# The order of the units in the product stage of a long-convolution block: early copies in the first group, whole pairs at the end of later groups

## The chip, the cores and the metric

The kernel runs on one core of a Trainium2 chip. The time is the device time of one execution in microseconds (us). Before the change it is 208.33 us, the median of three runs (207.98 to 208.43).

A core has TensorE (PE, matmuls, with its weight loads shown apart as PEld), VectorE (DVE), ScalarE (ACT), GpSimd (POOL) and SyncE (SP). Each takes its instructions in order, and semaphores tie the engines together. Matmuls write PSUM, eight banks per partition; ScalarE and VectorE read it.

## The reference

The block has two halves. The first is a gated long convolution over S = 2048 tokens and D = 512 channels, the second a dense ReLU layer pair with 1376 hidden units:

```python
k_shift = sum over 4 taps of shifted k * shift_k
kv = k_shift * v
y = irfft(rfft(kv padded to 2S) * rfft(ssm_k padded to 2S))[:S] + kv * ssm_D
h = x + layernorm(x) * y
out = h + relu(layernorm(h) @ w1) @ w2
```

The convolution is causal and runs along the tokens, for each channel by itself. What matters here is the product of the two spectra in the middle of it.

## The kernel before

The transforms are written as matmuls with tables of sines. The work goes in stages:

1. Tables, the four taps (`taps`) and a first transform step (`stage1`) of the filter into the tile `BK` and of `kv` into the tile `BX`. `stage1` runs 64 matmuls per call and casts the two PSUM buffers of a call out on ScalarE and VectorE (lines 273 and 275).
2. The product stage (lines 410 to 491). It carries out the second transform step of both and multiplies the two, and is the part that is changed.
3. The inverse transform (`inv1`, line 577, PSUM tile `psi`; then `inv2`, line 668, PSUM tile `pz`), with the weights `w1` centred beside it.
4. The dense layers, `mlp1` and `mlp2` (lines 680 and 696).

The product stage works in eight groups, c = 0 to 7, each with six units: four pairs u0 to u3 (`pairs`, line 437) and two sums s0 and s1 (`sums`, line 459). "Pair" is the kernel's own word for such a unit. A unit owns one PSUM buffer of two banks. In each of the two banks the left half takes the unit's transform K of the filter, from `BK`, and the right half its transform X of the data, from `BX`. A pair has a step K and a step X, of four matmuls each. A sum has four steps, K1, K2, X1 and X2, where 1 and 2 are two ways of assigning the array's row halves; a no-op on TensorE waits for the matmuls of one way before the other way begins.

`times(unit)` then multiplies the two: `forms` copies the K half out of PSUM to SBUF on ScalarE (line 423, tiles `ktu` and `kts`, two buffers each), and VectorE multiplies the X half, still in PSUM, with that copy (line 471). The product of a pair goes back into `BK`, into rows that neighbouring units' K steps read; the product of a sum goes into `BX`. So a product waits for all K steps that read its rows. Writing K and X below always means these halves; "copy u3" and "product u3" are the two instructions of `times` for u3.

There are four PSUM buffers of this kind. A new unit takes the one that was given back first, in the order of the products in the text, and its first matmul waits for that product.

The order of all this is written out by hand in two strings. A word such as `u3K` or `s0X1` is a step on TensorE, and a word such as `=u3` is the copy and the product of that unit. Each engine gets its instructions in the order of the string, and `FIRST` is for group 0, `OTHER` for groups 1 to 7:

```python
FIRST = "s0K2 u1K s1K2 s0K1 u0K s1K1 s0X1 u1X =u1 s0X2 =s0 s1X1 u0X =u0 s1X2 =s1 u2K u2X u3K =u2 u3X =u3"
OTHER = "s0K1 s0X1 u0K u0X s0K2 u1K =u0 s0X2 =s0 s1K1 s1X1 u1X =u1 s1K2 s1X2 =s1 u3K u2K u3X =u3 u2X =u2"
```

Beside the groups GpSimd makes the sum tables (`sum_tables`, line 383) for a group three later, and in three groups adds up rows of `w1` (line 416). At the end of the stage `column_means` runs four matmuls (line 500), and then the inverse transform begins.

Of the kernel before, what the change touches and what calls it, by code (L numbers as in the profile page):

```python
# [56 lines left out]
def kernel(  # L57
# [33 lines left out]
    early = pl.push("early", side="right")  # L91
# [287 lines left out]
    def sum_tables(c):  # L379
        ks = slice(4 * c, 4 * c + 4)  # L380
        for dp, pq in enumerate(halves):
            for i, op in ((0, ALU.subtract), (1, ALU.add)):
                nc.gpsimd.tensor_tensor(out=smc[pq, c % 3, i, :, 64 * dp:64 * dp + 64], in0=st[pq, ks, 64:128].bitcast(F32),  # L383
                                        in1=st[pq, ks, 0:64].bitcast(F32), op=op)
# [29 lines left out]
    def add_chunks(step):  # L414
        o, a, b = ((wsum, w1[:, 0, :], w1[:, 1, :]), (wpair, w1[:, 2, :], w1[:, 3, :]), (wsum, wsum.bitcast(F32), wpair.bitcast(F32)))[step]
        nc.gpsimd.tensor_tensor(out=o, in0=a, in1=b, op=ALU.add)
# [4 lines left out]
    def forms(ps, tag):  # L421
        kt = prod.tile([P, 2, 256], F32, tag=tag, name=tag, bufs=2)
        nc.scalar.copy(out=kt[:], in_=ps)  # L423
        return kt
# [40 lines left out]
                ways[way, dp] = last[dp]  # L465
        return do, ps, "kts", BXs[:, :, k1:k1 + 2, :].rearrange("p g k x -> p k g x")

    def times(unit):
        do, ps, tag, o = unit
        kt = forms(ps[:, :, 0:256], tag)  # L470
        nc.vector.tensor_tensor(out=o, in0=ps[:, :, 256:512].rearrange("p b (g x) -> p b g x", x=8),  # L471
                                in1=kt[:].rearrange("p b (g x) -> p b g x", x=8), op=ALU.mult)

    FIRST = "s0K2 u1K s1K2 s0K1 u0K s1K1 s0X1 u1X =u1 s0X2 =s0 s1X1 u0X =u0 s1X2 =s1 u2K u2X u3K =u2 u3X =u3"
    OTHER = "s0K1 s0X1 u0K u0X s0K2 u1K =u0 s0X2 =s0 s1K1 s1X1 u1X =u1 s1K2 s1X2 =s1 u3K u2K u3X =u3 u2X =u2"
    for c in range(8):
        units = {}
        for step in (OTHER if c else FIRST).split():  # L480
            if step[0] == "=":
                times(units[step[1:]])
                continue
            u = step[:2]
            if u not in units:
                units[u] = (pairs if u[0] == "u" else sums)(4 * c + (1 if u[0] == "u" else 2) * int(u[1]))
            units[u][0](step[2:])
        if c + 3 < 8:
            sum_tables(c + 3)
        if c in (2, 4, 5):  # L490
            add_chunks(max(c - 3, 0))
# [289 lines left out]
```

## Time and profile before

| what | value |
|---|---|
| median of three runs | 208.33 us |
| the profiled execution | 208.08 us |
| its span, first to last instruction | 206.3 us |
| mean granted TensorE clock | 0.994 |
| TensorE busy | 198.5 us, 96% of the span |
| VectorE, ScalarE, GpSimd busy | 69%, 57%, 34% |
| copies of line 423 | 48, 589 ns each |
| products of line 471 | 48, 685 to 688 ns each |

In a row of the timeline stand the start (us from the span's start), the time it took, engine, line, operation, what it writes and reads, the shapes and how many instructions were merged; in brackets the idle time of the engine before it and what ended it. The step of a row is found by its place in the string: in `OTHER`, a row `us<-BK` is s0K1, s0K2, s1K1 or s1K2, and `u<-BX` the X of a pair. Matmuls are pipelined: a row's time is longer than the distance to the next row, and it is the distance that counts.

### The profile page before, as it was taken

The page shows a single profiled execution, that of the slowest core. Times are in us where ns is not written, and L with a number is a line of the kernel's source. Part 1 is how long each engine was busy: PE and PEld are TensorE (multiplying, and loading weights), DVE is VectorE, ACT ScalarE, POOL GpSimd, SP SyncE. Part 2 cuts the span into 40 slices and gives each one's busy share as a digit, 9 for nine tenths or more (in the row PEclk, how much of TensorE's full clock was granted, in tenths as well). Part 3 has the DMA queues.
Part 4 walks back from the last instruction along what each step waited for, and adds up shares of the span by engine and source line. Part 5 has one row for each costly group of instructions (what it writes and reads, how often), then busy time and mean ns, then how long its engine had stood idle before and what let it go on. Part 6 is the DMA issues. An engine that isn't in the chain of part 4 may idle for free.

```text
span 206.3 us, 4591 instructions
## 1 busy us (share of the span) xinstructions
PE 198.5 (96%) x1861; PEld 139.0 (67%) x1869; DVE 142.5 (69%) x246; ACT 117.2 (57%) x190; POOL 69.4 (34%) x118
## 2 busy tenths in 40 slices
PE   8999999999999999999999999999999999999991
PEld 2575556877899999899998944466444844444460
DVE  5989898698689999997743775899098641361130
ACT  5776789787677877777691078404950065026300
POOL 7963801991557996032003032042102200002000
PEclk9999999999999999999999999999999999999997
DMA  5999970001700000035515999997906805110011
GB/s 161 344 209 191 214 122 3 0 5 22 257 0 3 0 3 3 0 108 98 101 39 176 277 195 105 204 148 135 124 12 130 142 25 105 29 57 16 0 51 51
DMA packets 47819, 19.93 MB, mean 97 GB/s; under 512 B 42710, under 2 KB 46264, under 8 KB 47800
## 3 DMA queue, kind: packets, MB, share of 16 engines
q1 hardware_dynamic: 44144, 16.15, 40.2%
q10 hardware_dynamic: 3656, 3.51, 5.6%
q8 instruction: 14, 0.23, 0.5%
q14 instruction: 5, 0.04, 0.1%
HBM read 7.02 MB, written 2.10 MB: 44 GB/s over the span
## 4 chain that ended last, share of the span: by engine, by line
PE 87%; DVE 7%; ACT 2%; DMA 1%; issue 1%; DVEq 0%; ACTq 0%
PE ps1m L680 19%; PE ps2m L696 18%; PE psi L577 11%; PE us L459 8%; PE ps L300 8%; PE u L437 7%; PE pz L668 7%; PE pkv L335 7%; PE pst L284 2%; DVE E L44 1%; DVE BK L471 1%; DMA wsh<-in_A_shift_k_dram 1%; DVE G L222 1%; DVE G L220 1%; ACT ktu L423 1%
## 5 line engine op out<-in xcount | busy, mean ns | idle before, releaser
L682 ACT ACTIVATE M<-ps1m 128x512 bf16<-128x512 f32 (+1 forms) x44 | 25.1, 595 | 49.4 <-PE ps1m L680 39.0
L696 PE MATMUL ps2m<-M 128*128 128x512 bf16 (+3 forms) x183 | 38.5, 366 | 0.2
L696 PEld LDWEIGHTS <-M 128*128 128x128 bf16 (+1 forms) x187 | 18.3, 98 | 19.9
L680 PEld LDWEIGHTS <-w 128*128 128x128 bf16 (+1 forms) x176 | 17.4, 100 | 19.9
L383 POOL TENSOR_TENSOR smc<-st 64x256 fp32r<-64x256 f32 x32 | 22.7, 730 | 10.8 <-PE us L459 10.0
L539 POOL TENSOR_SCALAR rstd<-mv 128x4 f32<-128x4 f32 x8 | 2.2, 276 | 70.1 <-DVE mv L537 70.1
L698 DVE SCALAR_TENSOR_TENSOR M<-ps2m,rstd,M 128x512 bf16<-128x512 f32 (+1 forms) x13 | 9.2, 707 | 23.2 <-PE ps2m L696 14.7
L471 DVE TENSOR_TENSOR BK<-u,ktu 128x512 fp32r<-128x512 f32 x32 | 21.3, 688 | 4.6 <-ACT ktu L423 3.3
L423 ACT COPY ktu<-u 128x512 f32<-128x512 f32 x32 | 18.1, 589 | 7.5 <-PE u L437 6.1
L577 PE MATMUL psi<-inv,BK 128*128 128x128 f32 x128 | 21.1, 255 | 0.0
L577 PE MATMUL psi<-inv,BX 128*128 128x256 f32 x64 | 20.5, 338 | 0.1
L577 PEld LDWEIGHTS psi<-inv,BK 128*128 128x128 f32 x128 | 19.7, 197 | 0.0
L680 PE MATMUL ps1m<-M,w 128*128 128x512 bf16 (+1 forms) x88 | 19.3, 379 | 0.0
L680 PE MATMUL ps1m<-xT,w 128*128 128x512 bf16 (+1 forms) x88 | 19.3, 379 | 0.0
L459 PE MATMUL us<-BK,smc 64*128 64x256 f32 x128 | 15.0, 313 | 0.4 <-ACT BX L273 0.4
L459 PE MATMUL us<-BX,smc 64*128 64x256 f32 x128 | 13.2, 284 | 0.0
L437 PE MATMUL u<-BK,st 64*128 64x256 f32 x128 | 12.9, 294 | 0.3 <-DVE BK L471 0.3
L577 PEld LDWEIGHTS psi<-inv,BX 128*128 128x128 f32 x64 | 12.1, 196 | 0.5 <-DVE BK L471 0.4
L535 DVE BATCH_NORM_STATS2 st<-M 128x6 f32<-128x512 bf16 x20 | 12.3, 678 | 0.0
L315 ACT CAST BK<-ps 128x512 fp32r<-128x512 f32 x16 | 9.3, 584 | 5.1 <-PE ps L300 3.4
L437 PE MATMUL u<-BX,st 64*128 64x256 f32 x128 | 11.9, 281 | 0.0
L654 DVE TENSOR_TENSOR qT<-pz,qT 128x2048 bf16<-128x2048 f32 x2 | 4.6, 2292 | 9.9 <-DMA qT<-M 5.8
(126 smaller groups left out, 408.4 us busy)
## 6 DMA issues: line engine op xcount, KB each, us to landing
E<-in_A_ssm_k_dram SPq DMA_DIRECT2D x1, 2048.0 KB
out_dram<-M ACTq DMA_DIRECT2D x15, 128.0 KB
w<-in_B_w_dram SPq DMA_DIRECT2D x1, 1376.0 KB
M<-in_B_w_dram ACTq DMA_DIRECT2D x1, 1280.0 KB
M<-in_A_q_dram SPq DMA_DIRECT2D x8, 128.0 KB
xh<-in_A_q_dram SPq DMA_DIRECT2D x4, 128.0 KB
xr<-in_A_q_dram SPq DMA_DIRECT2D x4, 128.0 KB
out_dram<-M ACTq DMA_DIRECT2D x2, 64.0 KB
```

The costliest lines, as they stand in the source:

```text
L300: nc.tensor.matmul(out=pss[rp][:, gi // 2, :, gi % 2, :], lhsT=fl[rows, 2 * g:2 * g + 2, :].rearrange("p d n -> p (d n)"), rhs=f[rows].rea ...
L335: nc.tensor.matmul(out=ps[:, i, :], lhsT=wdiag[:, r0 + i, j, :], rhs=kT[c][:, r0 + i, 16 - j:CH + 16 - j], start=(j == 0), stop=(j == KS - 1))
L383: nc.gpsimd.tensor_tensor(out=smc[pq, c % 3, i, :, 64 * dp:64 * dp + 64], in0=st[pq, ks, 64:128].bitcast(F32), in1=st[pq, ks, 0:64].bitcas ...
L423: nc.scalar.copy(out=kt[:], in_=ps)
L437: nc.tensor.matmul(out=ps[:, dp, 256 * x:256 * x + 256], lhsT=t[pq], rhs=cols((BK, BX)[x], pq, k1, i), start=not begun, stop=(i == 1), til ...
L459: mm = nc.tensor.matmul(out=ps[:, k % 2, 256 * x:256 * x + 256], lhsT=smc[pq, k // 4 % 3, i, k % 4, :], rhs=cols((BK, BX)[x], pq, k, i), s ...
L471: nc.vector.tensor_tensor(out=o, in0=ps[:, :, 256:512].rearrange("p b (g x) -> p b g x", x=8), in1=kt[:].rearrange("p b (g x) -> p b g x", ...
L577: nc.tensor.matmul(out=o if part == 0 else o[:, P * part - P:P * part], lhsT=src[:, g // 2, :, g % 2::2].rearrange("p c r -> p (c r)"), rh ...
L668: nc.tensor.matmul(out=pz[:, i, :, a:a + w, :].rearrange("p (s r) a n -> p s r (a n)", s=2), lhsT=ax[rho][:, n2 // 2, n2 % 2, :], rhs=ecor ...
L680: nc.tensor.matmul(out=ps1[:fsz, :].rearrange("p (i t) -> p i t", i=4), lhsT=w1[:, c, fc * P:fc * P + fsz], rhs=hT[sc][:, :, c, :], start= ...
L682: nc.scalar.activation(out=h1T[:fsz, fc, :], in_=ps1[:fsz, :], func=ACT.Relu)
L696: nc.tensor.matmul(out=ps2, lhsT=h1T[:ksz, fc, i * P:(i + 1) * P], rhs=w2[:ksz, fc, d0:d0 + w], start=(fc == 0), stop=(fc == NFC - 1))
```

## The change

`times` is split: `copy_k(unit)` is the copy alone, and `times` takes a copy that was made before. A new word `+u0` in the order makes that copy at its place, and the later `=u0` is then only the product.

In the first group the pairs u0 and u1 now go first with their K steps, and each is followed by its copy. The sums follow way by way as in later groups, and u3 goes ahead of u2. In later groups one thing is changed: u3X moves in front of u2K, so that the order at the end is u3K u3X u2K u2X, and copy and product u3 stand behind u2K. The numbers of matmuls, copies and products are the same.

```diff
-    def times(unit):
+    def copy_k(unit):
         do, ps, tag, o = unit
-        kt = forms(ps[:, :, 0:256], tag)
+        return forms(ps[:, :, 0:256], tag)
+
+    def times(unit, kt=None):
+        do, ps, tag, o = unit
+        kt = copy_k(unit) if kt is None else kt
         nc.vector.tensor_tensor(out=o, in0=ps[:, :, 256:512].rearrange("p b (g x) -> p b g x", x=8),
                                 in1=kt[:].rearrange("p b (g x) -> p b g x", x=8), op=ALU.mult)
...
-    FIRST = "s0K2 u1K s1K2 s0K1 u0K s1K1 s0X1 u1X =u1 s0X2 =s0 s1X1 u0X =u0 s1X2 =s1 u2K u2X u3K =u2 u3X =u3"
-    OTHER = "s0K1 s0X1 u0K u0X s0K2 u1K =u0 s0X2 =s0 s1K1 s1X1 u1X =u1 s1K2 s1X2 =s1 u3K u2K u3X =u3 u2X =u2"
+    FIRST = "u0K +u0 u1K +u1 s0K1 s0X1 u0X s0K2 =u0 u1X =u1 s0X2 =s0 s1K1 s1X1 u3K s1K2 s1X2 =s1 u2K u3X =u3 u2X =u2"
+    OTHER = "s0K1 s0X1 u0K u0X s0K2 u1K =u0 s0X2 =s0 s1K1 s1X1 u1X =u1 s1K2 s1X2 =s1 u3K u3X u2K =u3 u2X =u2"
     for c in range(8):
-        units = {}
+        units, early = {}, {}
         for step in (OTHER if c else FIRST).split():
+            if step[0] == "+":
+                early[step[1:]] = copy_k(units[step[1:]])
+                continue
             if step[0] == "=":
-                times(units[step[1:]])
+                times(units[step[1:]], early.pop(step[1:], None))
                 continue
```

## The prediction

> **What bounds the kernel now.** I read the page first (busy shares, then the chain that ended last), then the chain in order of time, then the product stage instruction by instruction, engine by engine. The page's rows of busy time and of the chain by engine:
>
> ```profile
> span 206.3 us, 4591 instructions
> PE 198.5 (96%) x1861; PEld 139.0 (67%) x1869; DVE 142.5 (69%) x246; ACT 117.2 (57%) x190; POOL 69.4 (34%) x118
> PE 87%; DVE 7%; ACT 2%; DMA 1%; issue 1%; DVEq 0%; ACTq 0%
> ```
>
> TensorE is on the chain for 87% of the span, so time that it loses inside the product stage counts. The stage runs from 49.6 us to 86.7 us; its end in the chain (start, us, what):
>
> ```profile
> 84.04 0.59 ACT ktu L423
> ...
> 84.65 0.69 DVE BK L471
> 85.34 0.60 DVE BX L471
> ...
> 85.96 0.70 DVE BK L471
> ...
> 86.71 23.23 PE psi L577 x192
> ...
> 109.96 0.29 DVE BX L275
> ...
> 110.60 7.64 PE pz L668 x64
> ```
>
> The stage ends not with a matmul but with copy u1, product u1, product s1, product u3 of the last group; the first inverse matmul at 86.71 waits for product u3, whose PSUM buffer it takes. From there TensorE runs without a break for 23.23 us and nearly so to the end. So what brings that point forward shortens the span one for one. One steady group, c=3, with the end of c=2 (timeline by engine; a step is 4 matmuls, that is two pairs; an x8 row is two steps):
>
> ```profile
> 61.96 0.41 PE L437 MATMUL u<-BX,st 64*128 64x256 f32 x4
> 62.20 0.50 PE L459 MATMUL us<-BK,smc 64*128 64x256 f32 x4
> 62.54 0.40 PE L459 MATMUL us<-BX,smc 64*128 64x256 f32 x4
> ...
> 63.27 0.65 PE L437 MATMUL u<-BX,st 64*128 64x256 f32 x8
> 63.87 0.51 PE L459 MATMUL us<-BK,smc 64*128 64x256 f32 x4
> ...
> 64.43 0.46 PE L437 MATMUL u<-BK,st 64*128 64x256 f32 x4
> 64.73 0.40 PE L437 MATMUL u<-BX,st 64*128 64x256 f32 x4
> 64.97 0.41 PE L459 MATMUL us<-BK,smc 64*128 64x256 f32 x4
> ...
> 65.69 0.50 PE L459 MATMUL us<-BK,smc 64*128 64x256 f32 x4
> 66.03 0.41 PE L459 MATMUL us<-BX,smc 64*128 64x256 f32 x4
> ...
> 68.17 0.48 PE L459 MATMUL us<-BK,smc 64*128 64x256 f32 x3
> ...
> 62.41 0.58 ACT L423 COPY ktu<-u 128x512 f32<-128x512 f32 x1 [0.26 <-PE u L437]
> 63.01 0.58 ACT L423 COPY kts<-us 128x512 f32<-128x512 f32 x1
> 63.72 1.08 ACT L423 COPY ktu<-u 128x512 f32<-128x512 f32 x2
> ...
> 63.03 0.69 DVE L471 TENSOR_TENSOR BK<-u,ktu 128x512 fp32r<-128x512 f32 x1 [0.15 <-ACT ktu L423]
> 63.64 0.68 DVE L471 TENSOR_TENSOR BX<-us,kts 128x512 fp32r<-128x512 f32 x1
> 64.34 1.29 DVE L471 TENSOR_TENSOR BK<-u,ktu 128x512 fp32r<-128x512 f32 x2
> ```
>
> A free-running step takes 0.24 us (64.73 to 64.97). Steps that take more follow a wait: s1K1 takes 0.34 (65.69 to 66.03), as does the change of way at 62.20. So a wait that ends late costs about 0.10 even when TensorE is not seen idle; the row's own length tells it, 0.50 for 0.41. There are four PSUM buffers, handed on in the order of the products: s0 of the next group takes u1's, u0 takes s1's, u1 takes u3's, s1 takes u2's. Read with that, the rows give a loop: u1X starts at 61.96; its copy at 62.41; product u1 at 63.03 to 63.72; s0K1 of the next group at 63.87, 1.91 after u1X began. Only from s0K1 to the next u1X does TensorE set its own pace, and there s1K1 loses 0.10 on product u2 (second of the two at 64.34, end 65.63). The group takes 68.17-63.87 = 4.30; 32 pairs at 0.12 would be 3.9.
>
> **Later groups (c=1 to 7): u3X goes ahead of u2K.** Nothing is added: same 64 matmuls, 6 copies, 6 products, no DMA, no GpSimd instruction; nothing moves past the queues of SyncE or GpSimd. u3X ends 0.24 earlier, u2K 0.24 later, u2X as before. Copy u3 waits for u3X (63.72 is 0.45 after the row at 63.27, as 62.41 is 0.45 after 61.96), so it is ready at 63.48. ScalarE's copies follow each other at about 0.48 (two in 1.08), so after copy s1 at 63.01 it starts at 63.49 and ends about 64.08. VectorE is then the one that is late: back to back its products follow at 0.61 (63.03, 63.64), so product u3 starts at 64.25 instead of 64.34: 0.09 earlier, not 0.24. Product u2 follows 0.61 later and ends at 65.54 instead of 65.63. u2K reads the rows of BK that product u3 writes, and so must be done first: it now ends about 63.7, well ahead of 64.25.
>
> s1K1 of the next group at 65.69 then has its buffer 0.15 ahead instead of 0.06. Is that enough to lose the 0.10? In c=3, u1K found its buffer free about 0.18 ahead (product u3 at 64.34 plus 0.69 is 65.03) and ran in 0.24:
>
> ```profile
> 65.21 0.41 PE L437 MATMUL u<-BK,st 64*128 64x256 f32 x4
> 65.45 0.41 PE L459 MATMUL us<-BX,smc 64*128 64x256 f32 x4
> ```
>
> u0K at 64.43 had 0.11 (product s1 ends 64.32) and took 0.30, a loss of 0.06. 0.15 lies nearer the first: I take 0.00 to 0.02 left of the 0.10. Bounds: all of it goes, or (as u0K) 0.06 stays. Once s1K1 is 0.10 earlier, u1X, its copy, its product and the next s0K1 are too: the loop hands it on. The steps that lost it, u1K of c=2 and s1K1 of c=2 and of c=7:
>
> ```profile
> 60.78 0.50 PE L437 MATMUL u<-BK,st 64*128 64x256 f32 x4
> 61.38 0.51 PE L459 MATMUL us<-BK,smc 64*128 64x256 f32 x4
> ...
> 82.99 0.51 PE L459 MATMUL us<-BK,smc 64*128 64x256 f32 x4
> ```
>
> s1K1 does so in all six groups from c=2 to c=7 (in c=1 it doesn't): 6 x 0.10 = 0.60. u1K of c=2, by the same 0.09 of product u3, adds 0.10. At the end, product u3 starts right behind product s1 with the same 0.09, so the psi stage starts 0.10 earlier still. Sum 0.80, between 0.40 and 0.90.
>
> **First group.** What was and is available (TensorE, ScalarE, VectorE; the first ACT row is the last cast of the stage before, the DVE row is product s1):
>
> ```profile
> 49.60 0.51 PE L459 MATMUL us<-BK,smc 64*128 64x256 f32 x4
> ...
> 50.74 0.76 PE L459 MATMUL us<-BK,smc 64*128 64x256 f32 x8 [0.39 <-ACT BX L273]
> ...
> 53.94 0.50 PE L437 MATMUL u<-BK,st 64*128 64x256 f32 x4 [0.31 <-DVE BK L471]
> ...
> 55.23 0.51 PE L459 MATMUL us<-BK,smc 64*128 64x256 f32 x4
> ...
> 55.79 0.46 PE L437 MATMUL u<-BK,st 64*128 64x256 f32 x4
> ...
> 49.68 1.01 ACT L273 CAST BX<-ps 128x1024 fp32r<-128x1024 f32 x1 [0.22 <-PE ps L300]
> 52.58 0.59 ACT L423 COPY ktu<-u 128x512 f32<-128x512 f32 x1 [1.88 <-PE u L437]
> ...
> 55.00 0.68 DVE L471 TENSOR_TENSOR BX<-us,kts 128x512 fp32r<-128x512 f32 x1
> ```
>
> Now u0K and u1K fill 49.60 to 50.2 (two steps, as before). The third unit still waits for the cast to 50.69, so the gap before 50.74 stays. ScalarE copies u0 at 50.71 to 51.30 and u1 to 51.78, in time in which it was idle (1.88 us). From here each pair is put 0.12 behind the last, and 0.10 is added where a wait has just ended. s0K1 50.74 and s0X1 51.09 run; u0X must wait for the copy of its own bank: 51.35 and 0.10 more. s0K2 51.69, u1X 51.94, s0X2 52.18, s1K1 52.42, s1X1 52.66, u3K 52.91 (buffer of u0, product from about 52.13 to 52.82; loses 0.07), s1K2 53.22, s1X2 53.47, u2K 53.71, u3X 53.95, u2X 54.19: TensorE ends at 54.43 where s0K1 stood at 55.23, 0.8 less. But VectorE gives only part of it on: product s1 needs s1X2 (53.59 for its last pair, 0.32 to the copy, 0.59 copy) and ends at 55.21 instead of 55.68, so u0K of c=1 waits until 55.27, where it stood at 55.79. It then loses 0.10 rather than the 0.06 of c=3, which leaves 0.48. s1K1 of c=1 had its buffer just in time; product u2, behind product s1 in VectorE's queue, comes nearly as much earlier, but the lead stays narrow, and up to another 0.10 goes there. I take 0.40.
>
> Bounds: the copy-before-X wait isn't shown in this trace in that direction. Below: u0X waits for both copies (51.78), 0.48 more, and the first group gains nothing. Above: no wait at all; what u0X gains is mostly lost again in u0K's wait for product s1, so 0.45. I take the value between, 0.40, where each X waits for its own unit's copy, because the copies of before wait for no more than their own unit's X.
>
> The Trainium skill bears on this (PSUM — Partial Sum Buffer, "PSUM bank collisions raise a hardware error"): guard PSUM by bank, not by address, since a matmul write and a read in one bank collide even in other columns. It speaks against an early copy: K and X of a unit share their banks, so X stands still while K is copied. The trace agrees in the direction that it shows: copies read K alone, yet each starts after X. By that rule the first group gains 0.40, by guarding addresses about 0.45.
>
> **Sum.** 0.80 + 0.40 = 1.20 us. The profiled execution took 208.08 us (span 206.3 and 1.8 around it): 206.9. The median of the runs is 0.25 above that execution, which would make it 207.1; I say 207.0.
>
> **Rivals.**
> (1) One part only. The wait at s1K1 stays because VectorE frees the buffer too late (0.06 left in six groups: 0.4 less), or the early units' X wait for both copies (0.4 less): 207.4. For it: the lead of 0.15 lies between two rows that decide differently.
> (2) No change. The stage ends earlier but the gain is lost before the end: the psi stage is followed at 109.96 by casts and at 110.60 by pz, which a DMA or a cast could hold. Against it: those casts wait for psi itself. Time 208.1.
> (3) Slower: X straight behind its own K, into the same two banks, restarts as a change of way does (62.20 to 62.54, 0.10 lost). Place: u3X and u2X in seven groups. From u1X to the next s0K1 TensorE has seven steps, 7 x 0.24 + 0.10 = 1.78 of the loop's 1.91, so 0.05 a step would cost nothing. At 0.10 a step they take 1.98, and each group loses most of what s1K1 gave: about 207.5. At 0.15 the gain of the first group goes too, about 208.2; from there it is slower, and at 0.20, 0.27 over the loop less the 0.10 of s1K1 in seven groups, less the first group's 0.40: 208.9. Against it: u0X stands behind u0K already and takes 0.24 (64.73 to 64.97).
>
> **How the numbers follow.** A measurement of this kernel can't tell less than about 0.2% (0.42 us) from no change. Forecast (both parts, 206.6 to 207.4): 0.62. Rival 1: 0.22, faster too. Rival 2: 0.08. Rival 3: 0.08. Faster 0.84, within 0.2% 0.08, slower 0.08. The range 206.4 to 207.8 holds the forecast with its upper bound (0.90+0.45) and a little spread below, and rival 1 with both losses (0.8 less) above; rivals 2 and 3 are left out.
>
> **What would show it.** s0K1 of c=1 near 54.5 and u0K of c=1 near 55.3; copy u3 of later groups starting about 0.49 behind copy s1, not 0.71; steps s1K1 at 0.24 in c=2 to 7; group length 4.20 instead of 4.31; psi from about 85.5 instead of 86.71, and still 23.2 long. Wrong if the s1K1 step stays at 0.34 (rival 1), if psi starts early and pz not (2), or if u3X or u2X take 0.34 (3).

## The result and the profile after

The changed kernel takes 207.38 us, the median of 20 runs (207.13 to 208.31), against 208.31 us for the kernel before (207.98 to 209.15). The ratio is 0.9963, with a 95% interval of 0.9953 to 0.9973: 0.4% faster, clear of no change. The profiled execution took 207.31 us, with a span of 205.2 us, 1.1 us less than before.

From the page of the changed kernel, its span and the chain that ended last by engine:

```profile
span 205.2 us, 4606 instructions
...
PE 90%; DMA 4%; ACT 2%; DVE 1%; issue 1%; SPq 0%
```

VectorE has gone from 7% of the chain to 1%, but most of that is not the change. Of VectorE's 14.1 us on the chain before, 10.4 lie ahead of the product stage, nearly all of them in the first 13 us; there the chain of the new profile runs over a DMA of 8.16 us instead, and the first `ps` matmuls start at the same moment (15.35 and 15.36). Within the product stage VectorE's part falls from 2.7 us to 0.7. The end of the stage and what follows it, in the chain in order of time (start, us, what):

```profile
83.57 0.97 PE u L437 x16
84.54 1.04 PE pm L507 x4
...
85.60 23.19 PE psi L584 x192
...
109.45 7.64 PE pz L675 x64
```

The inverse transform starts at 85.60 instead of 86.71, lasts as long as before, and `pz` starts 1.15 earlier. What was won before 85.60 is still there at the end. The stage now ends with TensorE's own matmuls (line 507) as the last link, where before it was copy u1 and three products. Product u3 ends at about 85.54 and those matmuls at 85.57, so this is a tie rather than a new bound.

A steady group of the changed kernel, c=3, with the end of c=2 (timeline of TensorE; the distance from row to row counts):

```profile
61.45 0.43 PE L437 MATMUL u<-BX,st 64*128 64x256 f32 x4
...
62.29 0.41 PE L437 MATMUL u<-BK,st 64*128 64x256 f32 x4
62.53 0.41 PE L437 MATMUL u<-BX,st 64*128 64x256 f32 x4
62.77 0.42 PE L437 MATMUL u<-BK,st 64*128 64x256 f32 x4
63.01 0.41 PE L437 MATMUL u<-BX,st 64*128 64x256 f32 x4
63.38 0.51 PE L459 MATMUL us<-BK,smc 64*128 64x256 f32 x4
...
65.20 0.41 PE L459 MATMUL us<-BK,smc 64*128 64x256 f32 x4
65.45 0.40 PE L459 MATMUL us<-BX,smc 64*128 64x256 f32 x4
...
67.60 0.51 PE L459 MATMUL us<-BK,smc 64*128 64x256 f32 x4
```

s1K1 (65.20) takes 0.25 where it took 0.34. u3K, u3X, u2K and u2X follow each other at 0.24. The group takes 67.60-63.38 = 4.22 instead of 4.30. Copies s1 and u3 of c=2 (timeline of ScalarE) show where the change acts: copy u3, the first of the second row, starts 0.48 behind copy s1, where it was 0.71.

```profile
62.52 0.59 ACT L423 COPY kts<-us 128x512 f32<-128x512 f32 x1
63.00 1.08 ACT L423 COPY ktu<-u 128x512 f32<-128x512 f32 x2
```

The loop itself is unchanged: from u1X at 61.45 to the next s0K1 at 63.38 are 1.93 us, and TensorE waits there, as s0K1 starts 0.37 behind u2X, where a step without a wait follows at 0.24.

### The profile page after: what moved, and what is told of

It reads as the page before. It is cut to its first block, busy times and chain, and to the rows that moved or that the text cites. A ratio compares the mean times of both kernels' runs of the same rounds, so it can differ in the third digit from the quotient of the medians.

```text
span 205.2 us, 4606 instructions
## 1 busy us (share of the span) xinstructions
PE 197.6 (96%) x1869; PEld 138.1 (67%) x1869; DVE 141.9 (69%) x246; ACT 116.4 (57%) x190; POOL 69.4 (34%) x118
## 4 chain that ended last, share of the span: by engine, by line
PE 90%; DMA 4%; ACT 2%; DVE 1%; issue 1%; SPq 0%
PE ps1m L687 19%; PE ps2m L703 19%; PE psi L584 11%; PE us L459 8%; PE ps L300 8%; PE pz L675 7%; PE u L437 7%; PE pkv L335 7%; DMA E<-in_A_ssm_k_dram 4%; PE pst L284 3%; PE pm L507 1%; ACT xfl L287 0%; ACT BX L273 0%; DVE BX L475 0%; DVE BK L312 0%
## 5 line engine op out<-in xcount | busy, mean ns | idle before, releaser
L459 PE MATMUL us<-BK,smc 64*128 64x256 f32 x128 | 14.5, 302 | 0.6 <-ACT BX L273 0.6
L437 PE MATMUL u<-BK,st 64*128 64x256 f32 x128 | 13.5, 290 | 0.2 <-DVE BX L475 0.2
L437 PE MATMUL u<-BX,st 64*128 64x256 f32 x128 | 13.0, 281 | 0.0
```

The costliest lines, as they stand in the source:

```text
L437: nc.tensor.matmul(out=ps[:, dp, 256 * x:256 * x + 256], lhsT=t[pq], rhs=cols((BK, BX)[x], pq, k1, i), start=not begun, stop=(i == 1), til ...
L459: mm = nc.tensor.matmul(out=ps[:, k % 2, 256 * x:256 * x + 256], lhsT=smc[pq, k // 4 % 3, i, k % 4, :], rhs=cols((BK, BX)[x], pq, k, i), s ...
```

## The experiments

The question was which of the two parts brings how much, whether the mechanism in each is the one that was named, and where the rest of the first group's time went. Each run was compared with the kernel before on the same chip.

**The two parts alone.** First the new `FIRST` with the old `OTHER`:

```diff
-    OTHER = "... =s1 u3K u3X u2K =u3 u2X =u2"
+    OTHER = "... =s1 u3K u2K u3X =u3 u2X =u2"
```

> The new order of the first group with the old order of the later groups. Theory of the prediction (two parts that add): TensorE ends the first group about 0.7 us earlier, VectorE's queue of products hands on about 0.3 of it (u0K of c=1 near 55.45 instead of 55.79), s1K1 of c=2 to 7 keeps its 0.34 us, the span is about 206.0 and the inverse transform starts near 86.4. Rival (the early copies bring nearly all of the 1.1 us of span): span 205.2 to 205.4. Rival (the first group's gain is lost again in later groups): span 206.3, as before.

Measured: 207.90 us, ratio 0.9978 (0.9968 to 0.9988), span 205.9. The opposite, the old `FIRST` with the new `OTHER`:

> The old order of the first group with u3X ahead of u2K in the later groups. Theory: s1K1 of c=2 to 7 takes 0.24 us, a group 4.24 instead of 4.31, the inverse transform starts near 85.9, the span is about 205.5 (0.8 less than before). Rival (all of it is the first group's): span 206.3 and groups of 4.31 us.

Measured: 207.53 us, ratio 0.9965 (0.9951 to 0.9979), span 205.4. The step s1K1 and the one behind it in c=3, and the start of the inverse transform, with the first group's order alone, from TensorE's timeline and from the chain:

```profile
65.40 0.51 PE L459 MATMUL us<-BK,smc 64*128 64x256 f32 x4
65.75 0.41 PE L459 MATMUL us<-BX,smc 64*128 64x256 f32 x4
```

```profile
86.40 23.18 PE psi L584 x192
```

and with the later groups' order alone, from the same two views:

```profile
65.45 0.41 PE L459 MATMUL us<-BK,smc 64*128 64x256 f32 x4
65.69 0.42 PE L459 MATMUL us<-BX,smc 64*128 64x256 f32 x4
```

```profile
85.83 23.22 PE psi L584 x192
```

The wait at s1K1 is there with the old order (0.35) and gone with the new (0.24). At the start of the inverse transform the first part is worth 86.71-86.40 = 0.31 us, the second 0.88; together 1.19, against 1.11 with both. They add up to within 0.1, as was held, and most comes from the later groups. That the early copies bring nearly all of it is refuted.

**Is it the earlier end of copy u3?** In the kernel before, with both old orders, copy u3 was made shorter instead of earlier in groups 1 to 7. The kernel then leaves out one bank's K, and product u3 takes the other bank's for both:

```diff
+        if half:
+            kt = prod.tile([P, 2, 256], F32, tag=tag, name=tag, bufs=2)
+            nc.scalar.copy(out=kt[:, 0, :], in_=ps[:, 0, 0:256])
+            k = kt[:, 0, :].rearrange("p (g x) -> p g x", x=8).unsqueeze(1).to_broadcast([P, 2, 32, 8])
+        else:
...
-                times(units[step[1:]])
+                times(units[step[1:]], c > 0 and step == "=u3")
```

> The kernel before, both orders old; in groups 1 to 7 copy u3 takes only one of its two banks (256 columns fewer, left out of the computation: product u3 uses one bank's K for both). Theory: what the new order of the later groups brings is nothing but an earlier end of copy u3, so that product u3 starts behind product s1 in VectorE's queue (0.09 us earlier) and s1K1 no longer waits. A copy that is 0.2 us shorter does the same with u3X where it was: s1K1 in 0.24, a group 4.24, the inverse transform near 85.85, span 205.4 as with the later groups' order alone. Rival (the gain is that X follows its own K, or that u2K comes later and no longer meets product s0): span 206.3, groups of 4.31.

Measured: 207.42 us, ratio 0.9960 (0.9943 to 0.9978), span 205.4. Its copies s1 and u3 (timeline of ScalarE, with line 423 for a whole copy and 472 for the half one):

```profile
62.78 0.58 ACT L423 COPY kts<-us 128x512 f32<-128x512 f32 x1
63.60 0.37 ACT L472 COPY ktu<-u 128x256 f32<-128x256 f32 x1 [0.24 <-PE u L437]
```

Its products s1 and u3 (timeline of VectorE):

```profile
63.41 0.68 DVE L477 TENSOR_TENSOR BX<-us,kts 128x512 fp32r<-128x512 f32 x1
64.01 1.29 DVE L477 TENSOR_TENSOR BK<-u,ktu 128x512 fp32r<-128x512 f32 x2
```

The step s1K1 and the one behind it (timeline of TensorE), and the start of the inverse transform (chain):

```profile
65.46 0.40 PE L459 MATMUL us<-BK,smc 64*128 64x256 f32 x4
65.70 0.41 PE L459 MATMUL us<-BX,smc 64*128 64x256 f32 x4
```

```profile
85.83 23.22 PE psi L582 x192
```

The copy starts no earlier than in the kernel before (0.82 behind the start of copy s1, there 0.71) but takes 0.37, and product u3 follows product s1 at 0.60. The inverse transform starts at 85.83, the same as with the later groups' new order. So the new place of u3X or u2K isn't itself what helps: it is that copy u3 ends before VectorE is free for its product.

**Is the loop what sets a group's length?** In the changed kernel copy u1 was made twice in groups 1 to 7:

```diff
+        if twice:
+            nc.scalar.copy(out=kt[:], in_=ps[:, :, 0:256])
...
+    TWICE = "=u1"
...
-                times(units[step[1:]], early.pop(step[1:], None))
+                times(units[step[1:]], early.pop(step[1:], None), c > 0 and step == TWICE)
```

> The changed kernel; in groups 1 to 7 ScalarE makes copy u1 twice, one behind the other (0.48 us more). Theory (a group's length is the loop u1X, copy u1, product u1, s0K1 of the next group): each group becomes 0.4 to 0.48 longer, 4.24 to about 4.67, span 208.2 to 208.6. Rival (TensorE's own steps or VectorE's queue set the length, and a copy on ScalarE, which is busy for under 3.6 of 4.3 us, is hidden): span 205.2 to 205.6.

Measured in one run: 211.2 us, span 209.4, 4.2 us more than the changed kernel, or 0.60 in each of seven groups. ScalarE's timeline, with copy u0, copy s0, the two copies u1 (lines 423 and 476) and copy s1:

```profile
65.87 0.59 ACT L423 COPY ktu<-u 128x512 f32<-128x512 f32 x1 [0.71 <-PE u L437]
66.60 0.59 ACT L423 COPY kts<-us 128x512 f32<-128x512 f32 x1
67.33 0.59 ACT L423 COPY ktu<-u 128x512 f32<-128x512 f32 x1
67.94 0.59 ACT L476 COPY ktu<-u 128x512 f32<-128x512 f32 x1
68.43 0.59 ACT L423 COPY kts<-us 128x512 f32<-128x512 f32 x1
```

TensorE's timeline, with u1X of the same group and s0K1 of the next:

```profile
66.87 0.41 PE L437 MATMUL u<-BX,st 64*128 64x256 f32 x4
69.40 0.51 PE L459 MATMUL us<-BK,smc 64*128 64x256 f32 x4 [0.58 <-DVE BK L477]
```

A copy that was held to be hidden by the rival, on an engine that still stands idle in every group (0.71 here), lengthens the kernel by all that it takes. All of it lies in the stretch from u1X to the next s0K1, 2.53 for 1.93 in the changed kernel; from s0K1 (64.57) to u1X (66.87) it is 2.30, for 2.31 there. The loop sets the length. The size was expected at up to 0.48 a group and is 0.60, so the span lies above the expected 208.2 to 208.6: the second copy starts 0.61 behind the first, which writes the same tile, while the copy behind it, into another tile, follows at 0.49.

**What the early copies bring.** The words `+u0` and `+u1` were taken out of the new `FIRST`:

```diff
-    FIRST = "u0K +u0 u1K +u1 s0K1 s0X1 u0X s0K2 =u0 ...
+    FIRST = "u0K u1K s0K1 s0X1 u0X s0K2 =u0 ...
```

> The changed kernel without the two early copies: in the first group the words +u0 and +u1 are taken out, so copies u0 and u1 are made where their products stand. Theory (the early copies matter, since ScalarE has nothing else to do from 50.7 us and copy u0 would else wait for u0X): product u0 starts about 0.2 us later than in the changed kernel, the whole row of products with it, span 205.4 to 205.5. Rival (the order alone brings the first group's gain, the early copies nothing): span 205.2, as the changed kernel. Rival (the bank wait makes an early copy a loss): span under 205.1.

Measured: 207.64 us, ratio 0.9974 (0.9958 to 0.9989), span 205.3; the inverse transform starts at 85.79, 0.19 later than in the changed kernel. The first product starts at 52.52 instead of 52.27 (rows of VectorE's timelines, first without and then with early copies):

```profile
52.52 1.29 DVE L475 TENSOR_TENSOR BK<-u,ktu 128x512 fp32r<-128x512 f32 x2 [1.59 <-ACT ktu L423]
```

```profile
52.27 1.29 DVE L475 TENSOR_TENSOR BK<-u,ktu 128x512 fp32r<-128x512 f32 x2 [1.32 <-PE us L459]
```

The direction and the size in the trace are those expected. The span of the profiled execution (205.3, expected 205.4 to 205.5) is a little below; over all 12 runs the median span is 205.45, against 205.15 over the 20 of the changed kernel, which were not taken beside them. In the times alone, 0.19 us can't be told from nothing. With the early copies the first product waits no longer for a copy but for the matmuls of s0K2, whose rows it overwrites.

**Does X wait for the copy of its bank?** In the changed kernel this can't be seen, since u0X comes late enough. So u0X was put right behind u1K:

```diff
-    FIRST = "u0K +u0 u1K +u1 s0K1 s0X1 u0X s0K2 =u0 ...
+    FIRST = "u0K +u0 u1K +u1 u0X s0K1 s0X1 s0K2 =u0 ...
```

> The changed kernel, with u0X in the first group put right behind u1K, ahead of s0K1 and s0X1, so that it meets copy u0 while that runs. Theory (X waits for the copy of its own banks): u0X starts 0.05 to 0.1 us after copy u0 ends (near 51.25, where BX is ready at 51.0), and s0K1, s0X1 follow it; span 205.6 to 205.9. Rival (the wait goes by address): u0X near 51.0, as soon as BX is ready. Rival (X waits for both copies): u0X near 51.75.

Measured in one run: 207.81 us, span 205.7. u0X in the timeline of TensorE, and copies u0 and u1 in that of ScalarE:

```profile
51.24 0.51 PE L437 MATMUL u<-BX,st 64*128 64x256 f32 x4 [0.96 <-ACT ktu L423]
```

```profile
50.59 1.08 ACT L423 COPY ktu<-u 128x512 f32<-128x512 f32 x2
```

Copy u0 runs from 50.59 to about 51.18, and u0X starts at 51.24; the profile names the copy as what ended the wait. Copy u1 ends at 51.67, so X waits for its own unit's copy alone. The data in `BX`, which u0X needs too, were complete at 50.95, when VectorE's last cast ended (48.50+2.45), so they don't account for the start at 51.24. The Trainium skill (PSUM — Partial Sum Buffer, "PSUM bank collisions raise a hardware error") asks for a guard by bank, since a write and a read collide there even in other columns. This kernel's waits agree with that rule: the copy reads the left half, u0X writes the right half, and it waits all the same. As both touch both banks of the buffer, a guard by whole buffer would look the same here. The cost in this place is 0.5 us of span against the changed kernel, as s0K1 and s0X1 stand behind u0X.

**The gap in front of the first group.** In the changed kernel TensorE idles from about 50.3 to 50.84, because two PSUM buffers are free and the two pairs in them have only one K step each. Two sums have four:

```diff
-    FIRST = "u0K +u0 u1K +u1 s0K1 s0X1 u0X s0K2 =u0 u1X =u1 s0X2 =s0 s1K1 s1X1 u3K s1K2 s1X2 =s1 u2K u3X =u3 u2X =u2"
+    FIRST = "s0K1 s1K1 s0K2 s1K2 u0K u0X u1K =u0 u1X =u1 s0X2 s1X2 s0X1 =s0 s1X1 =s1 u3K u3X u2K =u3 u2X =u2"
```

> The later groups as changed; the first group begins with all four K steps of the two sums, s0K1 s1K1 s0K2 s1K2, and then u0K u0X u1K =u0 u1X =u1 s0X2 s1X2 s0X1 =s0 s1X1 =s1 u3K u3X u2K =u3 u2X =u2, without early copies. Theory (in the first group what counts is the 0.5 us in which TensorE stands before 50.8 us, as two units have but two steps of K to give while two sums have four): the gap shrinks to under 0.2 us, the inverse transform starts near 85.1, span about 204.7. Rival (VectorE's queue alone sets when the second group starts, so filling the gap brings nothing): span 205.2.

Measured: 206.68 us (206.62 to 207.18), ratio 0.9928 (0.9913 to 0.9943), span 204.5. This is the fastest of all. Its first group, in the timelines of TensorE and then of VectorE:

```profile
49.68 1.32 PE L459 MATMUL us<-BK,smc 64*128 64x256 f32 x16
50.83 0.50 PE L437 MATMUL u<-BK,st 64*128 64x256 f32 x4
```

```profile
52.30 1.29 DVE L475 TENSOR_TENSOR BK<-u,ktu 128x512 fp32r<-128x512 f32 x2 [1.28 <-ACT ktu L423]
53.55 1.29 DVE L475 TENSOR_TENSOR BX<-us,kts 128x512 fp32r<-128x512 f32 x2
54.76 1.28 DVE L475 TENSOR_TENSOR BK<-u,ktu 128x512 fp32r<-128x512 f32 x2
```

16 matmuls now stand ahead of 50.83, where eight did. The first product comes no earlier than in the changed kernel (52.30 and 52.27). But now the six follow each other without a gap, since the sums' X steps come early enough, and the last ends at 56.04 instead of 56.58. The inverse transform starts at 85.02 (expected near 85.1, with a span of 204.7). The order differs from the changed kernel's in more than the filled gap: u3K, which has to wait for product u0, stands behind the sums instead of between their steps, and there are no early copies. How much of the gain each of these brings isn't separated.

## Why the prediction came out as it did

The forecast was 207.0 us: 1.20 less than the profiled execution is 206.9, and part of the 0.25 between that execution and the median was added. Measured are 207.38 in the median and a span 1.1 less. The direction, the mechanism of each part and the split were right. The first group's gain was off by 0.1, and what lies around the span, which the sum left as it was, grew by 0.3.

- **Later groups, 0.80 predicted.** Measured alone 0.88. Within the changed kernel it is 0.80: s0K1 of c=2 stands at 59.14 for 59.45 before, so 0.31 comes from ahead of it, and from there to the inverse transform it takes 26.46 instead of 27.26. The terms come out one by one: 0.18 in c=2, 0.38 in c=3 to 6, 0.24 in c=7 with the end, where 0.20, 0.40 and 0.20 were forecast. s1K1 was to go from 0.34 to 0.24 and a group to 4.20; measured are 0.25 and 4.22. Product u3 was to start behind product s1 in VectorE's queue. It does:

```profile
63.15 0.68 DVE L475 TENSOR_TENSOR BX<-us,kts 128x512 fp32r<-128x512 f32 x1
63.75 1.28 DVE L475 TENSOR_TENSOR BK<-u,ktu 128x512 fp32r<-128x512 f32 x2
```

  The two products of the second row end at 65.03, 0.17 ahead of s1K1 (65.20), which was the open point: 0.15 was forecast, between a row with 0.18 that lost nothing and one with 0.11 that lost 0.06.

- **First group, 0.40 predicted.** Measured alone 0.31. The step that failed is the list of TensorE's starts from 50.74 on:

```profile
50.84 0.51 PE L459 MATMUL us<-BK,smc 64*128 64x256 f32 x4 [0.57 <-ACT BX L273]
51.16 0.44 PE L459 MATMUL us<-BX,smc 64*128 64x256 f32 x4
51.41 0.44 PE L437 MATMUL u<-BX,st 64*128 64x256 f32 x4
51.66 0.51 PE L459 MATMUL us<-BK,smc 64*128 64x256 f32 x4
52.01 0.41 PE L437 MATMUL u<-BX,st 64*128 64x256 f32 x4
...
55.44 0.51 PE L437 MATMUL u<-BK,st 64*128 64x256 f32 x4 [0.22 <-DVE BX L475]
```

  s0K1 stood at 50.74 in the working and stands at 50.84. The 0.10 put on u0X for the wait for its copy isn't there (51.41 to 51.66 is 0.25); a loss of 0.10 sits one step later, at s0K2, where the way changes with only two pairs of matmuls between. These two cancel by luck, and the 0.10 at s0K1 stays, with a few hundredths more at u3K and s1K2. It goes through s1X2, copy s1 and product s1 to u0K of c=1: 55.44 where 55.27 was forecast. That VectorE would hand on only part of TensorE's lead was right: TensorE was 0.66 ahead at s0K1 of c=1 (54.57 for 55.23) and 0.35 at u0K (55.44 for 55.79).

- **The sum.** For the profiled execution 206.9 was forecast and 207.31 measured. Of the difference 0.1 is missing in the span, and 0.3 lies outside it: what lies around the span was taken as 1.8 us, unchanged, and is 2.1 in the profiled execution after. That isn't scatter of one execution. Over all runs of a kernel its median is 2.1 with the later groups' new order (the changed kernel and the runs with the later groups alone, without early copies and with the sums first; lowest 2.07), and 1.8 to 1.9 with the old one (the kernel before, the first group alone, the half copy; lowest 1.73 to 1.76). The single run with u0X moved fits with 2.1; the single run with copy u1 twice doesn't, at 1.8 with the new order. So about a quarter of what the span gained isn't in the time. What that part consists of stays open.

- **Rivals.** (1) One part only: refuted by the two halves, and its bank variant by u0X at 51.41, ahead of the end of copy u1. (2) Gain lost behind the stage: refuted, `pz` comes 1.15 earlier. (3) X behind its own K: refuted, u3X and u2X follow at 0.24 (62.29, 62.53, 62.77, 63.01).

## What to carry to other kernels

Where a steady loop looks bound by the busiest engine, look for steps that take a little longer than their like, and ask which release they meet: here 0.10 us in each of six groups came from a buffer that was free 0.06 us before its use, and 0.09 us at the right place removed it. A step moved ahead is worth what its slowest successor can hand on: u3X came 0.24 earlier and the product behind it 0.09, because VectorE's queue was next. And where an engine must wait for buffers anyway, try the units with most work for the free buffers in front: the order that does so was worth more than the early copies, 0.58 us at the start of the inverse transform against 0.19, though it moved u3K as well.

## What the runs showed that was not expected

In the changed kernel s0K1 of the first group starts 0.14 us after the end of the cast that frees its buffer (50.84 after 49.69+1.01), where in the kernel before the first matmul behind the same cast needed 0.05 (50.74 after 49.68+1.01). In front of s0K1 the trace has a semaphore instruction of 0.05 us on TensorE, at 50.7. There is one in each group, at the first step that uses a sum table; in the kernel before, that of the first group came already at 49.5, ahead of s0K2. This fits a step that waits for two things, a PSUM buffer and a table from GpSimd. That the second wait is what costs the 0.1 is not shown, as no run takes it away. The same delay stands in the loop of the steady groups: product u1 ends at 63.23 (62.54+0.69) and s0K1 starts at 63.38.

And two ScalarE copies into the same tile don't overlap, at 0.61 from start to start, while copies into different tiles do, at 0.48.
